# A RetNet and WaveMLP kernel on one core: the first half of a hand-written instruction order is laid out anew

## The chip, the cores and the metric

The kernel runs on one core of a Trainium2 chip. The metric is device time in microseconds for one execution. Before the change the median of three runs is 165.4 us (165.16 to 165.95). A core has five engines that run side by side, each through its own instruction list in order: TensorE (PE, matmuls and transposes into PSUM, with PEld for its weight loads), VectorE (DVE), ScalarE (ACT), GpSimd (POOL) and SyncE (SP). SP, ACT and POOL also issue DMA transfers.

## The reference

Two layers follow each other. The first is a linear recurrence with decay over 768 tokens, for 4 batches and 8 heads of 64 features; the second works on its output `x` of shape (4, 768, 512).

```python
for t in range(S):
    state = gamma * state + einsum('bhd,bhe->bhde', k[:, :, t], v[:, :, t])
    y[:, :, t] = scale * einsum('bhd,bhde->bhe', q[:, :, t], state)
...
theta = x @ w_theta
yr = einsum('ts,bsd->btd', w_tok_r, x * cos(theta))
yi = einsum('ts,bsd->btd', w_tok_i, x * sin(theta))
u = x + yr + yi
return u + maximum(u @ w_ch, 0.0)
```

Inputs and output are float32; the kernel multiplies in bfloat16 and sums in float32.

## The kernel before

The recurrence is computed in chunks of 128 tokens. The work is cut into 24 *units* n: a unit is half of the heads (4 of 8) and 256 tokens of one batch, so two units fill two chunks C of 128 tokens. Units 0 to 5 make batch 0, and so on. The 24 chunks also number the output tiles t.

The order of all instructions is written out by hand. `ORDER` is a string of 929 tokens such as `cqs.2.v`: a function's name, its numbers, and for many the engine (p POOL, v VectorE, a ACT) or the DMA queue (s SP, a ACT). The last lines of the kernel call the functions in that order, and each engine gets its instructions in the order in which they are called. An engine waits at an instruction until what it reads is there and the buffer that it writes is free. Nothing else moves instructions. The eight completion semaphores of the SP and ACT transfers are used in turn: the program makes each such transfer wait until the one eight places before it in the order has landed.

The steps of one unit n:

- `Lk`, `Lq`, `Lv` (L157) load k, q and v of the unit, 256 KB each, into 16 buffers for k and q and 9 for v.
- `ck` and `cq` or `cqs` (L302) turn k and q into bfloat16 `kqb`; `cqs` also scales q and is used for some units only. `cv` (L308) makes `vb`.
- `Tk`, `Tq` (L316) transpose both on TensorE, `E` copies the result out of PSUM as `kqT`. In later units `Dk` does the same by a DMA transpose.
- `A` (L346) multiplies keys and queries into `at_ps` (one buffer), `m` (L355, VectorE) applies the causal mask.
- `ST` (L373) adds up the unit's state change, `S0` and `S1` (L391, L395) keep the running state on VectorE, `SB` writes it as bfloat16 into block-diagonal tiles `sbd`.
- `I` (L411) takes the output from the older state, `Y` (L423) adds the one from inside the chunk, both into the PSUM banks of the next unit. `XB` and `XA` (L441) copy it out as `xT`.

The steps of the second layer, per chunk C or tile t:

- `Tx` (L455) with `Ex`, or `Dx`, turn `xT` into `x_sb`; `Hh` (L469) is the product with `w_theta`; `CN` (L476, ACT) takes sine and cosine; `z` (L483) multiplies them with `x`.
- `Tw` (L491) and `Ew` transpose the token-mixing weights, which `Pw` loads on POOL's queue in six pieces; `Pth` and `Pch` load the two other weights on the same queue, with a conversion to bfloat16 on the way.
- `M.t.s` (L509) is one pair of matmuls, and six such steps make a tile of `y`; `u` (L516) adds `x`; `Tu` and `Eu`, or `Du`, transpose; `O` (L536) is the product with `w_ch`; `f` (L542) finishes; `SO` stores.

`Z` (L278) is a filler: two matmuls of zeros whose result nobody reads.

The rotation of the PSUM buffers matters too: two banks for transposes, two for `th_ps`, `y_ps`, `o_ps` and the fillers, one for each half of the unit's output, and one for `at_ps`.

Of the kernel before, what the change touches and what calls it, by code (L numbers as in the profile page):

```python
# [29 lines left out]
ST.3 Lk.7.s S0.3.v SB.3.0.a S1.3 Lv.7.s Lk.8.s Tx.1 Tq.4 SB.3.1.p cv.4.p m.3 Pw.1.0 XB.2.0.a Ex.1.a  # L30
I.3 Lv.8.s E.4.a ck.5.a cq.5.a Y.3 Pw.0.0 ST.4 Hh.0 S0.4.v XB.3.0.v XB.3.1.v cv.5.v CN.0.1 A.4
CN.0.0 Tq.5 Hh.1 Tk.5 SB.4.0.p SB.4.1.a Pw.0.1 Hh.2 m.4 E.5.v I.4 Y.4 ST.5 ck.6.a Tk.6 Tx.2 cq.6.a
CN.1.1 CN.1.0 XA.4.1 A.5 XA.4.0 m.5 Lq.9.s Ex.2.v S0.5.v z.0.p Tq.6 E.6.a CN.2.0 cv.6.p Hh.3
SB.5.0.v Tx.3 Tw.1.0 z.1.v SB.5.1.a Ew.1.0.v Ex.3.a CN.2.1 A.6 I.5 Y.5 ST.6 XA.5.0 z.2.v Tw.0.0
CN.3.0 Tx.4 CN.3.1 Ew.0.0.v S0.6.v XA.5.1 Ex.4.v Hh.4 CN.4.0 CN.4.1 Tw.0.1 M.0.1 Pw.1.1 z.3.v M.0.0
Tw.0.2 Pw.1.2 Ew.0.2.a SB.6.1.a Hh.5 z.4.p SB.6.0.p Lk.9.a M.0.3 ck.7.p cqs.7.p M.0.2 CN.5.1 CN.5.0
cq.8.v m.6 Ew.0.1.v Tw.1.1 Tw.1.2 Ew.1.1.v Lv.9.s M.0.4 M.1.0 Tx.5 Ew.1.2.v M.1.1 S1.6 Tk.7 M.1.4
Pch Ex.5.v z.5.v cv.7.v Tq.8 Tq.7 M.1.2 E.7.a M.0.5 I.6 Y.6 ST.7 A.7 ck.8.a u.0 S0.7.v m.7 XA.6.1
SB.7.1.a M.1.5 M.1.3 XA.6.0 Tw.1.3 M.2.5 Pw.0.2 M.2.3 u.1 S1.7 Tk.8 M.2.1 M.2.0 SB.7.0.v Ew.1.3.a
Tu.0 I.7 cv.8.v E.8.a Lk.10.s ck.10.p cv.9.p Y.7 ST.8 A.8 cqs.9.v ck.9.v M.2.4 Du.1 Eu.0.a XB.7.1.a  # L40
XB.7.0.v S0.8.v SB.8.0.v M.2.2 Tx.6 Tq.9 Tk.9 Lv.10.a cv.10.p Lq.10.s S1.8 u.2 m.8 O.0 E.9.a
SB.8.1.a Hh.6 Tw.1.4 I.8 Y.8 A.9 CN.6.0 Du.2 Lq.14.s CN.6.1 Ex.6.v f.0 ST.9 Tw.0.3 Hh.7 Ew.1.4.v
Ew.0.3.a S0.9.v Tw.0.4 M.3.0 Tw.1.5 CN.7.0 CN.7.1 M.3.2 Dx.7 M.3.1 M.3.5 M.3.3 Lv.12.s Lk.12.s
Ew.1.5.v XA.8.1 Ew.0.4.v Lq.12.s M.3.4 u.3 S1.9 Tw.0.5 Tk.10 M.4.5 cqs.10.p XA.8.0 m.9 M.4.3 Tq.10
SB.9.1.a SB.9.0.a I.9 O.2 Lq.11.s Lk.11.s E.10.a Lk.15.s Ew.0.5.v Lk.14.s Y.9 ST.10 A.10 z.7.p
Lv.11.s XB.9.1.a XB.9.0.a f.2 M.4.0 O.1 M.4.1 cqs.14.p m.10 S0.10.v f.1 cq.11.a ck.12.v M.4.4 M.4.2
Tu.3 Eu.3.a Dx.9 SB.10.0.a cqs.12.p u.4 Hh.9 Tq.11 ck.11.v Tu.4 z.6.v Eu.4.v ck.15.v M.5.0 M.5.4
Tk.11 E.11.a SB.10.1.p cv.11.p M.5.2 M.5.3 I.10 M.5.5 M.5.1 Lq.13.a A.11 Y.10 ck.14.v ST.11 CN.9.1
CN.9.0 SO.0.a Hh.8 u.5 S0.11.v z.9.v XB.10.0.v m.11 Dk.12 Tx.8 Tq.14 O.4 Lv.13.a SB.11.0.a Lq.15.s
Lk.13.s CN.8.1 Lk.18.a XB.10.1.a CN.8.0 SB.11.1.p cv.12.p Lq.16.s I.11 Tk.14 Ex.8.v A.12 Y.11 ST.12  # L50
f.4 Lv.15.s O.3 z.8.p E.14.a XA.11.0 XA.11.1 Hh.10 S0.12.a f.3 SB.12.0.v Tx.10 Tu.5 CN.10.1 Dx.11
Ex.10.v cq.13.p Lk.16.s Lv.17.s Hh.11 SO.2.s CN.10.0 m.12 S1.12 z.10.v Tk.15 M.6.1 M.6.2 M.6.0 M.6.3
CN.11.0 CN.11.1 M.7.3 SB.12.1.a Lk.17.a ck.13.a M.7.4 M.7.0 M.6.4 Dk.13 M.7.1 z.11.v M.6.5 SO.3.s
A.14 M.7.2 Eu.5.v I.12 Lv.14.s u.6 cqs.15.v M.7.5 M.9.3 Tq.15 ck.17.a E.15.a m.14 SO.4.a Lq.17.s
Lq.18.s Lk.21.s ck.16.a M.9.0 M.9.5 M.9.1 M.9.4 Lq.19.a M.9.2 Du.6 cv.13.v u.7 M.8.0 u.9 Y.12
cv.14.p ST.13 A.13 O.5 XB.12.1.a XB.12.0.a M.8.1 S0.13.a S1.13 M.8.4 M.8.3 SB.13.0.a SB.13.1.p
cq.16.p m.13 I.13 ck.18.a Y.13 ST.14 A.15 f.5 cq.17.v Lv.18.a M.8.5 M.8.2 XA.13.0 XA.13.1 S0.14.v
SB.14.0.p Lv.16.s Hh.13 S1.14 u.8 Tx.12 M.10.1 cv.15.p cv.17.p SB.14.1.p M.10.0 M.10.4 cqs.18.v
M.10.5 CN.13.0 CN.13.1 Hh.12 CN.12.1 I.14 m.15 Y.14 CN.12.0 ST.15 S0.15.v XB.14.1.a SB.15.0.a M.10.3
cv.16.v Dk.16 Dk.17 Du.7 Dx.13 M.10.2 Dk.18 O.6 SB.15.1.p XB.14.0.v S1.15 I.15 Y.15 ST.16 SO.5.a  # L60
cv.18.p f.6 S0.16.v A.16 M.11.4 SB.16.1.p M.11.1 Lq.21.a Ex.12.a z.12.p SB.16.0.a Lk.19.s Lk.20.s
XB.15.0.a u.10 z.13.p XB.15.1.a m.16 O.7 Du.10 I.16 Y.16 ST.17 f.7 A.17 Tu.8 Hh.15 CN.15.1 CN.15.0
Dx.14 M.11.2 Tx.15 Lv.22.s SO.7.s M.11.0 M.11.5 S0.17.v SB.17.0.p M.11.3 XA.16.1 m.17 XA.16.0
Ex.15.v Hh.14 SB.17.1.p z.15.p cq.19.p ck.21.p Eu.8.a ck.19.p I.17 u.11 Tu.11 A.18 Y.17 ST.18
S0.18.v XA.17.1 XA.17.0 O.10 SO.1.a CN.14.1 S1.18 Lv.19.a CN.14.0 Dx.16 Lq.20.a f.10 Lq.22.a
SB.18.0.a Hh.17 SB.18.1.p Eu.11.v Tq.19 I.18 Tk.19 CN.17.1 O.8 Tx.17 CN.17.0 m.18 Hh.16 z.14.p
Lv.20.s Du.9 E.19.a f.8 O.11 Y.18 cv.19.p ck.20.a CN.16.1 ST.19 A.19 CN.16.0 M.12.1 Ex.17.v f.11
cq.20.p Lk.22.s Dk.20 M.12.0 S0.19.a M.13.3 M.13.2 XB.18.1.a SB.19.1.p SB.19.0.v M.13.0 z.17.v
cqs.21.v XB.18.0.v m.19 S1.19 z.16.v cv.20.v M.12.3 M.12.2 M.13.5 Lv.21.s M.13.1 M.12.4 M.12.5 I.19
M.13.4 Y.19 ST.20 u.12 A.20 Dk.21 XA.19.1 S0.20.v XA.19.0 ck.22.a cq.22.a SB.20.1.p cv.22.p M.14.3  # L70
M.14.5 M.14.1 M.14.4 M.14.2 M.14.0 SB.20.0.p u.13 m.20 S1.20 Hh.19 I.20 Y.20 SO.10.s Lq.23.s Lk.23.s
cv.21.v u.14 A.21 ST.21 CN.19.0 CN.19.1 S0.21.v M.15.3 M.15.5 S1.21 m.21 XA.20.1 Hh.18 CN.18.1
CN.18.0 Dx.18 Dk.22 ck.23.a M.15.4 M.15.2 SB.21.0.p M.15.1 M.15.0 SB.21.1.v Lv.23.s Du.12 Dx.19
XA.20.0 O.9 f.9 I.21 Y.21 A.22 ST.22 M.16.1 cqs.23.p u.15 m.22 S0.22.v z.18.p z.19.p M.16.5
SB.22.0.p M.16.4 O.12 M.16.0 SO.8.a M.16.2 M.16.3 SB.22.1.p XB.21.0.a XB.21.1.a SO.11.s Du.14
cv.23.p Dk.23 f.12 Du.13 Dx.20 Dx.21 Hh.21 u.16 I.22 A.23 Y.22 ST.23 CN.21.0 CN.21.1 Hh.20 CN.20.1
S0.23.v XA.22.1 XA.22.0 SB.23.0.a M.17.1 M.17.3 CN.20.0 M.17.0 SB.23.1.p I.23 M.17.2 m.23 Y.23 O.13
M.17.4 z.21.v M.17.5 Mh.0.1 Mh.0.3 XB.23.1.v f.13 Hh.23 u.17 XB.23.0.a SO.13.a CN.23.1 Du.16 Hh.22
z.20.v CN.22.1 Mh.0.2 M.19.3 Dx.23 CN.23.0 Dx.22 Mh.0.0 M.21.1 M.19.1 z.23.p CN.22.0 SO.6.a Du.17
M.18.1 O.16 M.21.2 M.19.2 M.19.0 M.18.3 f.16 SO.9.a M.18.5 z.22.p M.18.2 O.17 M.19.4 M.18.0 Mh.0.4  # L80
M.18.4 f.17 u.18 Du.15 SO.12.s O.15 M.19.5 f.15 u.19 SO.16.s M.22.2 M.22.1 O.14 Mh.0.5 uh.0 f.14
M.22.0 M.21.5 M.22.3 M.22.5 Du.19 M.21.4 SO.17.s M.22.4 Du.18 O.19 M.21.0 M.21.3 M.20.2 Mh.1.2
# [564 lines left out]
```

## Time and profile before

| what | value |
|---|---|
| median of three runs | 165.4 us |
| span of the profiled execution, first to last instruction | 163.6 us |
| TensorE busy | 155.2 us, 95% |
| VectorE busy | 114.0 us, 70% |
| ACT busy | 78.9 us, 48% |
| POOL busy | 74.3 us, 45% |
| bytes moved by DMA | 34.93 MB, 214 GB/s on average |
| read from and written to HBM | 25.69 MB and 6.29 MB |

The profile is of one execution. Its page gives each engine's busy time and share of the span, the busy share in 40 equal slices, the DMA queues, the chain of work that ended last, and the costliest groups of instructions. The trace behind the page answers finer questions: a timeline row has the start, the duration, the engine, the line, what is written and read, how many instructions were merged, and in brackets how long the engine stood idle before it and what released it. `SPq`, `ACTq` and `POOLq` are the issue of a DMA transfer. A row of the transfers has the tile, the queue, the count, the size and the time from issue to landing. Matmuls overlap, so the distance from start to start tells more of their cost than the duration.

### The profile page before, as it was taken

Reading aid. Unit: us, or ns where it says so; the run is one execution under the profiler, and the core shown is the slowest. Engines: PE = TensorE matmul, PEld = TensorE weight load, DVE = VectorE, ACT = ScalarE, POOL = GpSimd, SP = SyncE. Lnnn points to the kernel's source line nnn. Section 1 sums busy time; section 2 is a strip of 40 time slices with the busy share of each in tenths; the row PEclk is TensorE's granted clock in tenths of the full one; section 3 lists DMA queues with packets and bytes.
Section 4 is the critical chain, followed back from the end, with each engine's and each line's share of the span. In section 5 each row is a group of like instructions: output and inputs, shape, how many; then the busy total and the mean of one; then the engine's idle time right before and its main releaser. Section 6 shows DMA issues by size and latency. Waiting matters only on the chain.

```text
span 163.6 us, 4928 instructions
## 1 busy us (share of the span) xinstructions
PE 155.2 (95%) x2034; PEld 87.2 (53%) x2034; DVE 114.0 (70%) x215; ACT 78.9 (48%) x140; POOL 74.3 (45%) x107
## 2 busy tenths in 40 slices
...
GB/s 115 297 290 255 268 283 236 275 220 286 220 162 232 223 291 139 338 203 270 324 263 198 134 268 221 242 193 298 125 245 136 103 92 227 160 64 128 129 164 224
DMA packets 69062, 34.93 MB, mean 214 GB/s; under 512 B 26416, under 2 KB 66096, under 8 KB 69040
## 3 DMA queue, kind: packets, MB, share of 16 engines
q1 hardware_dynamic: 56032, 23.73, 69.4%
...
q0 software_dynamic: 2688, 3.41, 12.1%
q8 instruction: 16, 0.26, 0.7%
...
HBM read 25.69 MB, written 6.29 MB: 196 GB/s over the span
## 4 chain that ended last, share of the span: by engine, by line
PE 76%; DMA 8%; ACT 5%; POOL 3%; issue 2%; SPq 2%; DVE 1%; POOLq 0%; ACTq 0%
PE y_ps L509 36%; PE o_ps L536 11%; PE th_ps L469 10%; DMA kqf<-in_k_dram 8%; PE r_ps L423 3%; ACT qx L233 3%; PE w_ps L491 3%; PE at_ps L346 3%; PE r_ps L411 2%; PE kq_ps L316 2%; SPq L157 2%; PE y_ps L561 2%; ACT cs L476 1%; PE x_ps L455 1%; PE r_ps L373 1%
## 5 line engine op out<-in xcount | busy, mean ns | idle before, releaser
L509 PE MATMUL y_ps<-z,wtr 128*128 128x512 bf16 x138 | 52.4, 380 | 0.0
L509 PE MATMUL y_ps<-z,wti 128*128 128x512 bf16 x138 | 52.3, 379 | 0.0
L483 POOL TENSOR_TENSOR z<-cs,x_sb 128x1024 bf16<-128x1024 bf16 x12 | 25.5, 2136 | 17.9 <-ACT cs L476 10.0
L355 DVE TENSOR_TENSOR at<-at_ps,mask 128x1024 bf16<-128x1024 f32 x24 | 29.2, 1216 | 0.2
L469 PE MATMUL th_ps<-wth,xT 128*128 128x512 bf16 x96 | 24.5, 379 | 0.5 <-ACT cs L476 0.4
L516 DVE TENSOR_TENSOR u<-y_ps,x_sb 128x512 bf16<-128x512 f32 x23 | 15.8, 688 | 12.7 <-PE y_ps L509 12.6
L542 DVE SCALAR_TENSOR_TENSOR ot<-o_ps,u 128x512 f32<-128x512 f32 x22 | 15.1, 688 | 12.5 <-PE o_ps L536 12.4
L308 POOL TENSOR_TENSOR vb<-vf,vsc 128x512 bf16<-128x512 f32 x15 | 15.6, 1041 | 17.3 <-DMA vf<-in_v_dram 16.9
L476 ACT ACTIVATE cs<-th_ps,zerob 128x512 bf16<-128x512 f32 x24 | 16.4, 685 | 13.3 <-PE th_ps L469 8.8
L536 PE MATMUL o_ps<-wch,uT 128*128 128x512 bf16 x88 | 22.6, 379 | 0.0
L476 ACT ACTIVATE cs<-th_ps,halfpi 128x512 bf16<-128x512 f32 x24 | 16.3, 686 | 11.5 <-issue 5.4
L509 PEld LDWEIGHTS <-wtr 128*128 128x128 bf16 x138 | 13.5, 98 | 12.7
L509 PEld LDWEIGHTS <-wti 128*128 128x128 bf16 x138 | 13.5, 98 | 12.0 <-issue 0.2
L139 POOL CAST sbd<-s 64x256 bf16<-64x256 f32 (+1 forms) x21 | 10.1, 481 | 20.8 <-DVE s L391 17.7
L137 ACT COPY kqT<-kq_ps 128x1024 bf16<-128x1024 bf16 x12 | 12.1, 1012 | 11.9 <-PE kq_ps L316 11.9
L469 PEld LDWEIGHTS <-xT 128*128 128x128 bf16 x96 | 8.8, 98 | 8.7 <-issue 0.5
L137 ACT CAST kqb<-kqf 128x512 bf16<-128x512 f32 x16 | 9.6, 620 | 6.9 <-DMA kqf<-in_k_dram 6.3
L536 PEld LDWEIGHTS <-uT 128*128 128x128 bf16 x88 | 8.1, 98 | 8.3
L278 PE MATMUL zz<-zero 128*128 128x512 bf16 x30 | 10.3, 476 | 1.9 <-DVE zero L192 1.9
L423 PE MATMUL r_ps<-at,vb 64*64 64x128 bf16 x384 | 9.9, 221 | 1.6 <-DVE at L355 1.6
L316 PE MATMUL kq_ps<-ident,kqb 128*128 128x128 bf16 x120 | 11.2, 220 | 0.3 <-POOL kqb L302 0.3
L139 POOL CAST kqb<-kqf 128x512 bf16<-128x512 f32 x12 | 7.2, 612 | 8.5 <-DMA kqf<-in_k_dram 8.4
...
## 6 DMA issues: line engine op xcount, KB each, us to landing
vf<-in_v_dram SPq DMA_DIRECT2D x20, 256.0 KB, 5.9
kqf<-in_k_dram SPq DMA_DIRECT2D x19, 256.0 KB, 5.3
kqf<-in_q_dram SPq DMA_DIRECT2D x17, 256.0 KB, 5.8
out_dram<-ot ACTq DMA_DIRECT2D x12, 256.0 KB, 2.7
out_dram<-ot SPq DMA_DIRECT2D x11, 256.0 KB, 2.9
kqf<-in_q_dram ACTq DMA_DIRECT2D x7, 256.0 KB, 5.2
kqf<-in_k_dram ACTq DMA_DIRECT2D x5, 256.0 KB, 6.6
vf<-in_v_dram ACTq DMA_DIRECT2D x4, 256.0 KB, 5.8
```

Source lines behind the costliest of these rows:

```text
L137: nc.scalar.copy(dst, src)
L139: engines[e].tensor_copy(dst, src)
L308: engines[e].tensor_mul(in_blocks(vb), by_token(raw["vf", n]), _bcast_last(K["vsc"][:, i, :, h * HU:(h + 1) * HU], D))
L355: nc.vector.tensor_mul(at.rearrange("p g j a t -> p (g j) (a t)"), st["at_ps", n].rearrange("p g j a t -> p (g j) (a t)"), _bcast_mid(K["m ...
L423: nc.tensor.matmul(st["R", n + 1][c][g * D:(g + 1) * D, j * P:(j + 1) * P], st["vb", n][rows, lo:lo + D], st["at", n][rows, g, j, a, :], s ...
L469: nc.tensor.matmul(th_ps, st["xT", C][:, j, :], K["wth"][:, j, :], start=(j == 0), stop=(j == 3))
L476: nc.scalar.activation(st["cs", C][:, w, :], st["th_ps", C], AF.Sin, bias=K["zerob" if w else "halfpi"], scale=1.0)
L483: engines[e].tensor_mul(st["z", b][:, c], st["cs", C], _bcast_mid(x_of(C), 2))
L509: nc.tensor.matmul(st["y", t], K["wT"][r][:, s0, t0 * P:(t0 + 1) * P], st["z", b][:, s0, r, :], start=(done == 0 and r == 0), stop=(done = ...
L516: nc.vector.tensor_add(st["u", t], st["y", t], st["x", b][:, t0, :])
L536: nc.tensor.matmul(o_ps, st["uT", t][:, j, :], K["wch"][:, j, :], start=(j == 0), stop=(j == nD - 1))
L542: nc.vector.scalar_tensor_tensor(st["ot", t], st["o", t], 0.0, st["u", t], ALU.max, ALU.add)
```

## The change

The first 538 of the 929 tokens are put in a new order; the last 391, from `M.10.1` on, stay as they were. The same tokens stand in both halves, but 80 of them name another engine: the conversions, copies and products that may run on VectorE, ACT or POOL. The queue of each transfer is kept: a load that SP issued is still issued by SP, at another place in the order. The new order was laid out over a replay of the kernel in which the transfers of all queues are served in the order of their issue.

The beginning of the diff, up to unit 7 or so:

```diff
 const2 Lv.0.s const1 const6.v Z.29 Z.2 const5 Z.38 Lk.0.a const3 Z.35 Z.8 Lq.0.s Lv.1.s Z.28 constA
-const4 Lq.1.a const9 Lk.1.s Z.39 const8 ck.0.p Tk.0 ck.1.a cqs.0.v cv.0.p Tq.0 E.0.v Lq.4.a ST.0
-Lk.4.a cqs.1.p Tq.1 Lq.2.s S0.0.v SB.0.1.v A.0 Lk.2.s SB.0.0.p cv.1.p Lv.2.s S1.0 Z.15 I.0 Z.27 m.0
-Tk.1 E.1.a cqs.2.v Z.34 cv.2.p Y.0 ST.1 XB.0.1.a S0.1.v S1.1 SB.1.0.a Pth Lq.3.s Z.18 XB.0.0.v Tq.2
-A.1 SB.1.1.a ck.2.a I.1 m.1 Y.1 ST.2 Tk.2 const7 Z.23 XB.1.0.v Lk.3.s E.2.v XB.1.1.v A.2 ck.3.p
-S0.2.v m.2 S1.2 SB.2.1.a Z.11 cqs.3.p Tq.3 Lv.3.s Tx.0 Tk.3 Z.3 ck.4.p Lv.4.s Lk.5.s Lq.5.s Lv.5.s
-Lq.6.s Lk.6.s Lv.6.s Lq.7.s E.3.a SB.2.0.v I.2 Y.2 XB.2.1.a Ex.0.a cv.3.v cq.4.p Tk.4 Lq.8.s A.3
...
+const4 Lq.1.a const9 Lk.1.s cv.1.v Lk.2.s cv.0.p ck.1.a ck.0.p Z.39 ST.0 Tk.0 S0.0.v Lk.4.a cqs.0.v
+SB.0.0.v S1.0 Tq.0 E.0.a Lk.3.s Lq.2.s cqs.1.v Tq.1 ck.2.a A.0 cqs.2.p Tk.1 SB.0.1.v Pth I.0 Lq.4.a
+const8 ck.3.a Tk.2 Lq.5.s Z.18 m.0 const7 E.1.v Tq.2 ck.4.p Lq.3.s Y.0 E.2.v A.1 Z.34 ST.1 Z.23 m.1
+cqs.3.p Tk.4 XB.0.1.a XB.0.0.v Lv.3.s Lv.2.s cv.2.p S0.1.v Pw.1.0 A.2 Lk.5.s Z.11 Lv.4.s Tk.3 SB.1.0.a
+S1.1 SB.1.1.a Tq.3 cq.4.a I.1 Y.1 m.2 Lv.5.s ST.2 XB.1.1.v Tq.4 S0.2.v Lk.6.s S1.2 E.3.a XB.1.0.v Z.3
+SB.2.1.p cv.3.p Tx.1 A.3 Lq.6.s SB.2.0.a m.3 Lv.6.s Lq.7.s E.4.a Z.15 Ex.1.a I.2 Y.2 ST.3 cq.5.p Tx.0
+S0.3.v Hh.1 Lk.7.s SB.3.0.a SB.3.1.p S1.3 Pw.0.0 XB.2.0.v XB.2.1.v Hh.0 I.3 Y.3 CN.1.1 Ex.0.v cv.4.v
+ST.4 Pw.0.1 A.4 Tq.5 CN.1.0 Pw.1.1 ck.5.v Lv.7.s Tk.5 XB.3.0.v S0.4.v CN.0.0 cv.5.p m.4 XB.3.1.a
+SB.4.1.a Hh.2 E.5.a z.1.v SB.4.0.p Tx.2 I.4 Y.4 CN.0.1 ST.5 Pw.1.2 XA.4.0 Pw.0.2 ck.6.p S0.5.v Ex.2.a
+cq.6.a SB.5.1.p A.5 Tw.1.0 CN.2.1 Z.27 Lk.8.s Tk.6 XA.4.1 Tq.6 SB.5.0.p Ew.1.0.v Lq.8.s E.6.a Tx.3 m.5
...
+Ew.1.2.v cv.7.p ck.8.p Tq.7 z.4.v Tk.7 Tw.1.1 M.2.2 m.6 Lq.10.s SB.6.0.v M.2.1 M.2.0 M.0.4 M.2.5 M.2.4
+I.6 E.7.a Tw.1.4 Ew.1.1.a M.2.3 Tw.1.5 u.0 M.1.0 Lk.9.a M.1.1 cqs.9.p Ew.1.4.v Y.6 ST.7 A.7 Ew.1.5.a
+M.1.3 u.2 Tu.0 S0.7.v Tw.0.4 SB.7.0.a M.1.5 SB.7.1.v Lv.10.a Lq.11.s cq.8.a Eu.0.v Du.2 Tk.8 Ew.0.4.a
+Tq.8 cv.9.p M.1.2 S1.7 XA.6.1 I.7 M.4.2 cv.8.v E.8.a XA.6.0 M.1.4 m.7 u.1 Tw.0.3 M.4.1 M.4.3 Y.7 ST.8
...
```

The order in which the transfers are issued changes with it. Before, the loads of SP and ACT come as k0, v0, q0, v1, q1, k1, then q2, k2, v2, q3, k3, v3 with q4 and k4 on ACT's queue between them, then v4, k5. After, they come as k0, v0, q0, v1, q1, k1, k2, k3, q2, q5, q3, v3, v2, k5, v4 with k4 and q4 on ACT's queue. POOL issues `Pth` behind `cqs.2`, and five of the six `Pw` pieces within a few steps after `Pw.0.0`, `Pw.0.2` among them, which before came behind `Pch`.

More of the change, by code (lines that the diff above doesn't have):

```diff
@@ L29 @@
-Lq.6.s Lk.6.s Lv.6.s Lq.7.s E.3.a SB.2.0.v I.2 Y.2 XB.2.1.a Ex.0.a cv.3.v cq.4.p Tk.4 Lq.8.s A.3
[L30 to L82, printed above, removed]
```

50 lines of the change are left out of this document (46 added, 4 removed).

## The prediction

> **What bounds the kernel now.** I read the page first, then TensorE's order in time up to 30 us, then the busy time on both sides of the place where the two orders become equal, then the transfers.
>
> ```profile
> span 163.6 us, 4928 instructions
> PE 155.2 (95%) x2034; PEld 87.2 (53%) x2034; DVE 114.0 (70%) x215; ACT 78.9 (48%) x140; POOL 74.3 (45%) x107
> PE 76%; DMA 8%; ACT 5%; POOL 3%; issue 2%; SPq 2%; DVE 1%; POOLq 0%; ACTq 0%
> ```
>
> TensorE is busy for 95% of the span and holds 76% of the chain that ended last. The change only permutes work, so its gain can come only from gaps on TensorE. They all lie early:
>
> ```profile
> 7.34 0.61 PE L316 MATMUL kq_ps<-ident,kqb 128*128 128x128 bf16 x8
> ...
> 9.70 0.59 PE L278 MATMUL zz<-zero 128*128 128x512 bf16 x2
> 10.13 0.39 PE L316 MATMUL kq_ps<-ident,kqb 128*128 128x128 bf16 x4
> ...
> 13.86 0.42 PE L423 MATMUL r_ps<-at,vb 64*64 64x128 bf16 x16 [1.11 <-DVE at L355]
> ...
> 15.56 0.42 PE L346 MATMUL at_ps<-kqT 64*64 64x128 bf16 x16 [0.39 <-DVE kqT L139]
> ...
> 17.79 0.38 PE L411 MATMUL r_ps<-kqT,sbd 128*128 128x128 bf16 x4 [0.17 <-DVE sbd L139]
> 18.10 0.42 PE L423 MATMUL r_ps<-at,vb 64*64 64x128 bf16 x16
> 18.45 0.40 PE L316 MATMUL kq_ps<-ident,kqb 128*128 128x128 bf16 x4
> 18.78 0.42 PE L346 MATMUL at_ps<-kqT 64*64 64x128 bf16 x16
> 19.03 0.29 PE L373 MATMUL r_ps<-vb,kqb 64*64 64x64 bf16 x16
> 19.48 0.38 PE L455 MATMUL x_ps<-ident,xT 128*128 128x128 bf16 x4 [0.16 <-ACT x_sb L137]
> 19.70 0.39 PE L316 MATMUL kq_ps<-ident,kqb 128*128 128x128 bf16 x4
> 20.42 0.38 PE L411 MATMUL r_ps<-kqT,sbd 128*128 128x128 bf16 x4 [0.33 <-ACT xT L137]
> 21.27 0.42 PE L423 MATMUL r_ps<-at,vb 64*64 64x128 bf16 x16 [0.47 <-DVE at L355]
> 21.49 0.32 PE L373 MATMUL r_ps<-vb,kqb 64*64 64x64 bf16 x16
> 21.75 1.04 PE L469 MATMUL th_ps<-wth,xT 128*128 128x512 bf16 x4
> ...
> 26.94 0.40 PE L316 MATMUL kq_ps<-ident,kqb 128*128 128x128 bf16 x4
> 27.72 1.02 PE L469 MATMUL th_ps<-wth,xT 128*128 128x512 bf16 x4 [0.39 <-ACT cs L476]
> ```
>
> ```profile
> 28.63:87.06 58.43, 58.34 (x829) 34.55 (x828) 46.50 (x93) 32.99 (x58) 22.28 (x25) 1.00 1.22 246
> ```
>
> The first answer shows the real matmuls starting at 7.34, ahead of them only seven filler steps (Z). The seven gaps marked from 13.86 on sum to 1.11 + 0.39 + 0.17 + 0.16 + 0.33 + 0.47 + 0.39 = 3.02 us. The second has one stage, from 28.63 to 87.06, where the common tail of the two orders begins (token M.10.1): TensorE busy 58.34 of 58.43 us, at the full granted clock (1.00). Were all seven gaps gone, the gain would be 3 us. The loads are what the early gaps depend on:
>
> ```profile
> 1.86 0.50 SPq L157 DMA_DIRECT2D vf<-in_v_dram  x1
> vf<-in_v_dram SPq DMA_DIRECT2D x1, 256.0 KB, 6.1
> ...
> 9.32 6.61 DMA kqf<-in_k_dram
> ...
> 15.94 0.37 SPq L157
> ...
> 12.62 0.93 POOL L173 DMA_DIRECT2D wth<-in_moe_w_theta_dram  x1
> wth<-in_moe_w_theta_dram POOLq DMA_DIRECT2D x1, 512.0 KB, 6.8
> q1 hardware_dynamic: 56032, 23.73, 69.4%
> q0 software_dynamic: 2688, 3.41, 12.1%
> ```
>
> Lv.1, fifth load in the order of issue, lands at 1.86 + 6.1 = 7.96. Lk.4, the fourteenth, issued by ACT at 9.32, lands at 15.93. That is (15.93 - 7.96) / 9 = 0.89 us a load, so the transfers are a second full resource. The step after it shows the limit on depth: SP issues Lk.5 at 15.94, as the load eight places before it has landed. Weights cost more: queue 0 takes 12.1 / 3.41 = 3.55% a MB, queue 1 takes 69.4 / 23.73 = 2.92%, or 1.21 times as much, so Pth (512 KB) occupies the engines for 2 x 0.89 x 1.21 = 2.2 us.
>
> **The change, part by part.** *Conversions moved between engines.* No matmul, copy or load is added; 80 copies and products change engine and both halves hold the same 14 filler steps. TensorE sees only when operands are ready, so I price waits.
>
> *Start.* VectorE's first product is now cv.1 and its second work on unit 0 comes behind it; cqs.0 used to be first.
>
> ```profile
> 6.22 0.69 DVE L302 TENSOR_TENSOR kqb<-kqf,qsc 128x512 bf16<-128x512 f32 x1 [3.26 <-DMA kqf<-in_q_dram]
> 10.56 1.01 ACT L137 COPY kqT<-kq_ps 128x1024 bf16<-128x1024 bf16 x1 [1.09 <-PE kq_ps L316]
> 11.63 1.04 POOL L308 TENSOR_TENSOR vb<-vf,vsc 128x512 bf16<-128x512 f32 x1 [1.34 <-DMA vf<-in_v_dram]
> 8.85 0.62 ACT L137 CAST kqb<-kqf 128x512 bf16<-128x512 f32 x1
> ```
>
> VectorE must sit until Lv.1 at 7.96, is done with cv.1 at 8.65 (0.69 us for that shape), copies S0.0 and ends cqs.0 near 9.5. Tq.0 thus starts near 9.6 where TensorE is free near 7.8: some 1.7 us idle, and 0.8 us more until Tq.1 behind cqs.1. E.0 moves to ACT: 10.0 to 11.0. This start alone isn't the cost, because fillers stand in the old order there (Z.15 and Z.27 have run by 10.13) and later chains bind; it counts through the ledger below.
>
> *Loads.* Lv.2 goes from ninth to fourteenth place, Lq.4 from twelfth to fifteenth: ACT issues it behind ck.2, which stands behind E.0, so near 11.0. Pth keeps its time: cqs.2 on POOL needs Lq.2, ninth, at 7.96 + 4 x 0.89 = 11.5, takes 1.05 and frees POOL at 12.6. Then POOL does ck.4, cqs.3 and cv.2. Served in order, Lv.2 lands at 15.93 and cv.2 ends at 15.95 + 1.04 = 17.0; Lq.4 lands at 15.93 + 0.89 = 16.8. If Pth goes ahead of them, both slip by up to its 2.2 us: Lq.4 to 19.0. Which end is nearer is shown by another load issued just before POOL's transfers:
>
> ```profile
> 20.86 1.10 SPq L157 DMA_DIRECT2D kqf<-in_q_dram  x1
> kqf<-in_q_dram SPq DMA_DIRECT2D x1, 256.0 KB, 9.7
> 21.28 0.60 POOL L182 DMA_DIRECT2D row<-in_moe_w_tok_i_dram  x1
> ```
>
> Lq.7, 0.4 us ahead of three weight transfers, took 9.7 us, not 6.1: it was overtaken. Lq.4 would have 1.6 us of lead over Pth, so I take a little over half of the slip: 18.1.
>
> The Trainium skill (DMA: Bandwidth & Descriptors, Queues, rings and completion order) states that each DMA engine takes turns between the queue rows that have work, a packet at a time, which speaks against an order laid out over service in issue order. By that rule Lq.4, alone on ACT's row, would pass Lv.2, and Lv.2 would share with Pth and land near 18.1: cv.2 to 19.15, ST.2, Tq.4, Z.3 and Tx.1 behind it, A.3 near 20.3, an estimate 0.5 us worse than mine. Lq.7's row agrees for POOL's queue; for SP against ACT the even 0.89 us steps don't show it.
>
> *Who waits for Lq.4.* ACT holds cq.4, then E.3, then SB.2.0; A.3 on TensorE waits for E.3. cq.4 runs 18.15 to 18.8, E.3 to 19.8, A.3 starts at 19.85. Before it started at 18.78. TensorE has done less by then: the order puts Z.15, Z.27, I.2 and Y.2 after A.3, Tq.4 before it. From start to start a Z takes 10.13 - 9.70 = 0.43, I.2 0.31, Y.2 0.35, a Tk or Tq 0.33: 0.86 + 0.31 + 0.35 - 0.33 = 1.19 us. So the new order is 1.07 + 1.19 = 2.26 us behind at A.3.
>
> *What it wins back.* The gaps after 18.78 in the old order, start to start: ST.3 to Tx.1 0.45 where 0.26 is needed (21.49 to 21.75), Tq.4 to I.3 0.72 for 0.33, I.3 to Y.3 0.85 for 0.31, Tq.6 to Hh.3 0.78 for 0.33: 0.19 + 0.39 + 0.54 + 0.45 = 1.57. The new order sets Tx.0, Hh.1 and Hh.0 before I.3, two groups of four long matmuls (21.75 to 22.71 is one, 0.96 us), which cover the two largest. I leave 0.2 us of loss (0 if the cover is whole, 1.57 if nothing is covered).
>
> **Sum:** 2.26 - 1.57 + 0.2 = +0.9 us on a span of 163.6; nothing after 87.06 differs but the start time. The median 165.4 lies 1.8 us over that span and keeps its distance: 166.3.
>
> **The rivals.**
> *Served in issue order, faster.* Lq.4 at 16.8 gives cq.4 to 17.45, E.3 to 18.45, A.3 at 18.5: -0.28 + 1.19 - 1.57 = -0.66 with no loss left, so 164.7; with the 0.2 us tightening elsewhere that the rows can't tell, 164.5. For it: the fourteen even landings, of both queues. Against it: Lq.7's 9.7 us. It decides at a landing of Lq.4 before about 17.
> *Weights drawn ahead starve unit 8, clearly slower.* Pw.0.2 (576 KB) is now issued before Lk.8, Pch (512 KB) soon after.
>
> ```profile
> 27.08 0.97 SPq L157 DMA_DIRECT2D kqf<-in_k_dram  x1
> kqf<-in_k_dram SPq DMA_DIRECT2D x1, 256.0 KB, 12.7
> ...
> 38.26 0.61 PE L316 MATMUL kq_ps<-ident,kqb 128*128 128x128 bf16 x8
> ```
>
> Lk.8 landed at 39.8 behind the same loads as Lq.8 in the new order; Pw.0.2 adds 2.25 x 0.89 x 1.21 = 2.4 us, Pch up to 2.2: 42.2 to 44.4. TensorE ran Tq.8 at 38.26; the new order has about 6 us more ahead of it (eight M steps net, 0.43 each, and ten short ones), so with 0.9 us of delay it comes at 45 and cq.8 needs the load by 44.4. It decides from there; some 1.7 us late gives 168.0. For it: 12.7 us for one load. Against: the margin, 0 to 2 us.
> *Nothing comes of it.* The start's loss and the cover cancel (the slip of Lq.4 is 0.4 of Pth's): 165.4.
>
> **How the numbers follow.** Forecast 0.48, own range 164.7 to 167.2 (Lq.4 in order, or wholly behind Pth); in order 0.26; starved 0.17; nothing 0.09. A measurement of this kernel tells about 0.5%, 0.8 us, from no change. The forecast lies just beyond it: 0.31 slower, 0.17 same. In order: 0.17 faster, 0.09 same; starved: slower; nothing: same. Slower 0.48, same 0.35, faster 0.17. The range 164.3 to 168.1 takes in both sides.
>
> **What would show it.** Tq.0 idle until about 9.6 behind VectorE's cv.1; Lq.4 landing near 18; cq.4 or E.3 as the releaser ahead of A.3 near 19.9; no gaps from 20 to 28; M.10.1 starting near 88.0. Wrong if Lq.4 lands before 17, if a gap over 0.5 us stands before Tq.8, or if M.10.1 comes before 87.

## The result: slower by 0.6%, and the profile after

The changed kernel takes 166.74 us (median of five, 166.41 to 166.78); the ratio to the kernel before is 1.0059, 95% interval [1.0037, 1.0082]. The forecast was 166.3 us. The two medians, 165.4 and 166.74, are 1.3 us apart, the two profiled spans 1.4. All ratios go by the faster state of the executions; in `e10_all_early` seven of twelve, at 168.3 to 168.6 us and at a granted clock of 0.99 to 1.00, fell out as slow, so its ratio may flatter it and stands alone. Lines in `kernel.py` are two lower than before (the loads L155, `ck`/`cq` L135 or L137, `cqs` L300, `cv` L306, `Tk`/`Tq` L314, `A` L344, `ST` L371, `Y` L421).

First the page of the changed kernel: the span, the engines' busy times, the granted clock in 40 slices, and the queue that brings instructions (transfers, MB, share), which is needed near the end.

```profile
span 165.0 us, 4914 instructions
PE 154.0 (93%) x2005; PEld 87.6 (53%) x2034; DVE 112.1 (68%) x211; ACT 78.7 (48%) x138; POOL 77.8 (47%) x113
PEclk9978999999999999999999999999999999999998
q8 instruction: 16, 0.26, 0.7%
```

TensorE's busy time is 1.2 us less over a span that is 1.4 us longer, but 29 of its 2,034 matmul records are missing, so this difference proves little. The work is the same by construction. Where TensorE loses time is shown by its order in time, each row with start, duration, line, tiles and, in brackets, the idle time and what ended it:

```profile
9.47 0.40 PE L314 MATMUL kq_ps<-ident,kqb 128*128 128x128 bf16 x4 [1.22 <-DVE kqb L300]
10.39 0.51 PE L314 MATMUL kq_ps<-ident,kqb 128*128 128x128 bf16 x4 [0.53 <-DVE kqb L300]
...
18.89 0.39 PE L453 MATMUL x_ps<-ident,xT 128*128 128x128 bf16 x4
19.21 0.42 PE L344 MATMUL at_ps<-kqT 64*64 64x128 bf16 x16
...
32.87 0.28 PE L453 MATMUL x_ps<-ident,xT 128*128 128x128 bf16 x2 [0.77 <-issue]
...
45.94 0.40 PE L314 MATMUL kq_ps<-ident,kqb 128*128 128x128 bf16 x4 [0.86 <-ACT kqb L135]
```

Two gaps at the start (Tq.0, Tq.1), A.3 at 19.21 with no wait marked before it, then a gap in the middle of Tx.4 that no semaphore explains, and one before Tq.8. The one before Tq.8 ends with cq.8 on ACT, and the chain of waits, cut at 50 us and followed back, says what cq.8 waited for (start, duration, what):

```profile
26.00 19.25 DMA kqf<-in_q_dram
45.27 0.63 ACT kqb L135
45.94 0.40 PE kq_ps L314 x4
```

Lq.8 was on its way for 19.25 us. The transfers that SP and POOL issued around it, as rows of the transfers (tile, queue, count, size, us from issue to landing):

```profile
kqf<-in_k_dram SPq DMA_DIRECT2D x1, 256.0 KB, 16.7
row<-in_moe_w_tok_r_dram POOLq DMA_DIRECT2D x1, 576.0 KB, 14.2
kqf<-in_q_dram SPq DMA_DIRECT2D x1, 256.0 KB, 19.2
wch<-in_moe_w_ch_dram POOLq DMA_DIRECT2D x1, 512.0 KB, 11.2
```

These are Lk.8 (issued at 25.46, landed at 42.2), Pw.0.2 (26.18, 40.4), Lq.8 (26.00, 45.2) and Pch (33.23, 44.4). Pch was issued 7 us after Lq.8 and landed 0.8 us before it (44.4 against 45.2).

A ledger says what each stage cost. For every TensorE step I take the distance from the start of its first matmul to the next such start, less the distance that this kind of step needs where nothing waits (M and Z 0.43, Hh and O 0.86, Tw 0.335, A, Y and ST 0.235, the others 0.22, an I of two matmuls 0.11), and add up from 6.5 us:

```
TensorE time lost since 6.5 us, at the start of   A.3    A.6    M.0.1  Tq.8   M.10.1 (starts at)
before                                            4.08   6.72   7.26   7.29   8.73   (87.06)
after                                             5.61   6.82   7.88   9.05   10.16  (88.50)
```

The change is 1.53 us behind at A.3 and has made up all but 0.10 us by A.6, at 30 us. The order of the small steps differs, so such a difference is sure to 0.1 or 0.2 us only. Between A.6 and Tq.8 the change loses 2.23 us where the kernel before lost 0.57: 0.94 at Tx.4's gap and 1.03 at Tq.8's. From Tq.8 to M.10.1 it loses 1.11 where the kernel before lost 1.44. The sum, 0.10 + 1.66 - 0.33 = 1.43 us, is the delay of M.10.1 (88.50 - 87.06), and behind M.10.1 both take the same 76.5 us.

### The profile page after: what moved, and what is told of

Read it like the earlier page. It is cut to its first block, busy times and chain, and to the rows that moved or that the text cites. A ratio compares the mean times of both kernels' runs of the same rounds, so it can differ in the third digit from the quotient of the medians.

```text
span 165.0 us, 4914 instructions
## 1 busy us (share of the span) xinstructions
PE 154.0 (93%) x2005; PEld 87.6 (53%) x2034; DVE 112.1 (68%) x211; ACT 78.7 (48%) x138; POOL 77.8 (47%) x113
## 4 chain that ended last, share of the span: by engine, by line
PE 74%; DMA 15%; POOL 3%; issue 2%; DVE 2%; ACT 2%; SPq 1%; POOLq 0%; DVEq 0%; ACTq 0%
PE y_ps L507 31%; DMA kqf<-in_q_dram 12%; PE o_ps L534 11%; PE th_ps L467 10%; PE r_ps L421 4%; PE kq_ps L314 4%; DMA vf<-in_v_dram 4%; PE at_ps L344 3%; PE r_ps L409 3%; PE y_ps L559 2%; PE r_ps L371 2%; PE zz L276 2%; PE x_ps L453 1%; POOL z L481 1%; POOL kqb L137 1%
## 5 line engine op out<-in xcount | busy, mean ns | idle before, releaser
L507 PE MATMUL y_ps<-z,wtr 128*128 128x512 bf16 x133 | 50.5, 380 | 0.5
L507 PE MATMUL y_ps<-z,wti 128*128 128x512 bf16 x126 | 47.8, 379 | 0.8 <-issue 0.6
L481 POOL TENSOR_TENSOR z<-cs,x_sb 128x1024 bf16<-128x1024 bf16 x11 | 23.4, 2134 | 10.1 <-ACT cs L474 9.9
L306 POOL TENSOR_TENSOR vb<-vf,vsc 128x512 bf16<-128x512 f32 x17 | 18.0, 1061 | 13.0 <-DMA vf<-in_v_dram 8.4
L467 PE MATMUL th_ps<-wth,xT 128*128 128x512 bf16 x90 | 23.7, 379 | 0.3
L137 POOL CAST sbd<-s 64x256 bf16<-64x256 f32 (+1 forms) x23 | 10.5, 456 | 27.9 <-DVE s L389 27.0
L135 ACT CAST kqb<-kqf 128x512 bf16<-128x512 f32 x19 | 11.6, 624 | 5.5 <-DMA kqf<-in_k_dram 4.1
L314 PE MATMUL kq_ps<-ident,kqb 128*128 128x128 bf16 x120 | 11.4, 230 | 2.8 <-DVE kqb L300 1.8
L300 POOL TENSOR_TENSOR kqb<-kqf,qsc 128x512 bf16<-128x512 f32 x8 | 8.8, 1094 | 8.8 <-DMA kqf<-in_q_dram 8.8
L135 ACT COPY kqT<-kq_ps 128x1024 bf16<-128x1024 bf16 x11 | 11.1, 1011 | 3.7 <-PE kq_ps L314 3.6
L314 PEld LDWEIGHTS <-kqb 128*128 128x128 bf16 x120 | 8.5, 103 | 6.9 <-DVE kqb L300 2.1
```

Of the source, the lines that this page charges most:

```text
L135: nc.scalar.copy(dst, src)
L306: engines[e].tensor_mul(in_blocks(vb), by_token(raw["vf", n]), _bcast_last(K["vsc"][:, i, :, h * HU:(h + 1) * HU], D))
L314: nc.tensor.transpose(st["kq_ps", n][:, 4 * w + x, :], st["kqb", n][:, w, x * P:(x + 1) * P], K["ident"])
L467: nc.tensor.matmul(th_ps, st["xT", C][:, j, :], K["wth"][:, j, :], start=(j == 0), stop=(j == 3))
L481: engines[e].tensor_mul(st["z", b][:, c], st["cs", C], _bcast_mid(x_of(C), 2))
L507: nc.tensor.matmul(st["y", t], K["wT"][r][:, s0, t0 * P:(t0 + 1) * P], st["z", b][:, s0, r, :], start=(done == 0 and r == 0), stop=(done = ...
```

## The experiments

Theory A, formed on these rows: the weight transfers Pw.0.2 and Pch, drawn ahead, starve unit 8's loads. The edits are moves of tokens in `ORDER`.

**One transfer moved.** `e1_pch_later` puts Pch behind cv.7:

```diff
-z.5.v Tw.1.2 cqs.7.p Lq.9.s Pch Lv.9.s ck.7.a ... cv.7.p ck.8.p Tq.7
+z.5.v Tw.1.2 cqs.7.p Lq.9.s Lv.9.s ck.7.a ... cv.7.p Pch ck.8.p Tq.7
```

> Pch is issued behind cv.7 instead of ahead of it, some 5 us later (near 39 us instead of 33.2); all else as in the changed kernel (median 166.74, span 165.0, Lq.8 landing at 45.24, 0.9 us of idle TensorE before Tq.8). Theory A (weights drawn ahead of unit 8's loads make Lq.8 late): Lq.8 lands near 43.2, the gap before Tq.8 goes, the time falls by 0.9 to 1.2 us to about 165.7. Rival B (the transfers as a whole set the pace, so another load takes Lq.8's place): Lq.8 lands earlier but a gap of the same size opens elsewhere before 60 us, for O.0 or a later unit, and the time stays within 0.3 us of 166.74.

Measured: 166.07 us, ratio 1.0041 [1.0013, 1.0069], executions from 165.06 to 167.48. Lq.8, in the rows of the transfers of this kernel (issued at 25.84), and Pch (39.66):

```profile
kqf<-in_q_dram SPq DMA_DIRECT2D x1, 256.0 KB, 15.7
wch<-in_moe_w_ch_dram POOLq DMA_DIRECT2D x1, 512.0 KB, 8.7
```

Lq.8 lands at 41.6 instead of 45.2, Tq.8 follows Tk.8 without a wait, and M.10.1 starts at 87.72. The starving is shown: one transfer taken out of Lq.8's way gives it 3.5 us. The other runs repeat it. In the four profiles with this order's engines and Pch at its early place (the changed kernel, e2, e3, e4) Lq.8 lands at 45.0 to 45.7 and Tq.8 waits 0.86 to 1.67 us; in the six with Pch later (e1, e5, e9 to e12) it lands at 41.2 to 41.8 and Tq.8 doesn't wait. What that is worth in time is not as sure: the interval overlaps that of `e4_after_again` below, and the median is above the 165.7 that theory A had forecast.

**The start.** `e2_cqs0_first` puts cv.1 behind cqs.1 on VectorE; `e3_fillers_early` puts three fillers into TensorE's first gaps; `e4_after_again` is the changed kernel once more.

```diff
 e2
-Lk.1.s cv.1.v Lk.2.s ... cqs.0.v ... cqs.1.v Tq.1
+Lk.1.s Lk.2.s ... cqs.0.v ... cqs.1.v cv.1.v Tq.1
 e3
-Tk.0 S0.0.v ... Tq.0 E.0.a ... Z.18 ... Z.34 ... Z.23
+Tk.0 Z.18 Z.34 S0.0.v ... Tq.0 Z.23 E.0.a
```

> cv.1 goes behind cqs.1 on VectorE, so that cqs.0 no longer waits behind Lv.1. The two gaps of 1.2 and 0.5 us before Tq.0 and Tq.1 should go in either theory and the granted clock should stay at 1.00 from 10 to 14 us, where it was 0.50. Theory C (the loss at the start is carried to the end): A.3 starts about 1 us earlier than 19.2, M.10.1 too, and the time falls by about 1 us to 165.7. Rival D (the loss at the start is absorbed before 31 us, since both orders are equally far there; what costs is later): A.3 moves by less than 0.5 us and the time by less than 0.4 us.

> The fillers Z.18 and Z.34 go into the gap before Tq.0 and Z.23 into the one before Tq.1, from behind Tk.2 and A.1; the wait for cqs.0 stays. If idle TensorE is what lowers the granted clock, the clock stays at 1.00 from 10 to 14 us. Theory C': the half clock delays the unit chain (Tq.2, Y.0, A.1) and its end is worth 0.5 us or more, time 166.2 or less. Rival D': the chain is bound by VectorE and the loads there, or what is won is absorbed by 31 us, time within 0.3 us of 166.74.

> The changed kernel once more, unchanged, beside the others. The 0.77 us of idle TensorE in the middle of Tx.4 at 32.1 us had no releaser in the profile. If it belongs to the order (a fixed place in TensorE's instruction stream), it stands again at the same instruction with 0.5 us or more; if it was chance, it is gone or stands elsewhere. The time is 166.4 to 166.8 either way.

Measured: e2 166.78, ratio 1.0086 [1.0063, 1.0109]; e3 166.76, 1.0072 [1.0046, 1.0099]; e4 166.64, 1.0063 [1.0042, 1.0084]. In e2 Tq.0 starts at 8.31 instead of 9.47, with gaps of 0.66 and 0.53 us left before Tq.0 and Tq.1, and A.3 still at 19.20; in e3 A.3 comes at 19.58. The start as such is absorbed. The clock was 1.00 from 10 to 14 us in both, as expected, but in e3 it was 0.50 from 15.2 to 18.5 instead, and e1 kept 1.00 with the old start, so nothing is shown about what the fillers do to the clock. e4 gives the same two late gaps in other sizes, 0.34 us at Tx.4 (less than the 0.5 forecast) and 1.40 before Tq.8, and M.10.1 at 88.31.

**Lv.2.** What holds TensorE before A.3 in e1 is ST.2, waiting for cv.2, and so for Lv.2, now in fourteenth place:

```profile
18.11 0.32 PE L371 MATMUL r_ps<-vb,kqb 64*64 64x64 bf16 x16 [0.99 <-POOL vb L306]
```

`e5_lv2_early` is e1 with Lv.2 issued three places earlier.

```diff
-ck.3.a Tk.2 Lq.5.s ... Lq.3.s ... Lv.3.s Lv.2.s cv.2.p
+ck.3.a Tk.2 Lv.2.s Lq.5.s ... Lq.3.s ... Lv.3.s cv.2.p
```

> This is the kernel of e1_pch_later with one more load moved: SyncE issues Lv.2 ahead of Lq.5, Lq.3 and Lv.3, in place of behind them. Theory (what holds ST.2 and A.3 in the changed kernel is Lv.2's late place among the loads, landing at 16.81): Lv.2 now lands at 13.5 to 15, the first product of A.3 starts at 18.4 to 18.9 in place of 19.21. What that is worth: if early lateness persists, the median is 165.1 to 165.4 (0.7 below e1); rival (lateness of that stage is made up by 30 us, because the loads of units 4 to 6 or the weights of that stage bind anyway): the ledger is level with e1 again by A.6 and the median stays within 0.3 of 166.07.

Measured: 167.02, ratio 1.0114 [1.0077, 1.0152]. Lv.2 lands at 12.3 and the wait is gone, but A.3 starts at 19.14 against e1's 19.34 and A.6 at 29.84 against 29.99, and 0.16 us of that lead was there at Tk.0 already (7.27 against 7.43). So taking the wait away bought next to nothing, as the rival said, but not for the rival's reason, and the median isn't within 0.3 of e1's as the rival had it. The granted clock of the two kernels from 10 to 14 us (stretch, length, busy time of PE, PEld, DVE, ACT and POOL, then the clock, the DMA share and GB/s), e1:

```profile
10.00:14.00 4.00, 3.23 (x69) 2.00 (x70) 3.05 (x6) 3.98 (x8) 1.91 (x2) 1.00 1.22 290
```

and e5:

```profile
10.00:14.00 4.00, 3.50 (x60) 2.44 (x64) 2.84 (x5) 3.98 (x8) 1.92 (x2) 0.71 1.22 290
12.00:15.00 3.00, 3.00 (x42) 1.53 (x40) 2.46 (x4) 2.98 (x5) 1.96 (x3) 0.50 1.22 290
```

In e5 TensorE ran at half its clock from 12 to 15 us and reached A.2 later than in e1, e5 first:

```profile
16.24 0.42 PE L344 MATMUL at_ps<-kqT 64*64 64x128 bf16 x16
```

```profile
15.26 0.42 PE L344 MATMUL at_ps<-kqT 64*64 64x128 bf16 x16
```

The dip cost the microsecond that Lv.2 gave. The changed kernel had the same dip (0.57 over 10 to 14). There TensorE came to ST.2 at 17.98 without a wait, just when cv.2 had ended (17.92), so the dip and Lv.2 would each have set that time alone. In the profile e5 falls behind e1 at O.0, which waited 0.76 us for Pch (landed at 49.2).

**Order and engines apart.** `e6_old_engines` is the new order with the 80 tokens' old engines, `e7_new_engines_old_order` the reverse.

```diff
 e6
-cv.1.v Lk.2.s cv.0.p ... E.0.a ... cqs.1.v
+cv.1.p Lk.2.s cv.0.v ... E.0.v ... cqs.1.p
```

> The new order with the vector steps on the engines that they had before (80 steps given back their old engine; order, loads and weights as in the changed kernel). Theory A (the loss is the order of the transfers: Pw.0.2 and Pch ahead of unit 8's loads): Lq.8 still lands at 44.5 to 46, a gap of 0.5 to 1.7 us before Tq.8 remains, and the median is 166.4 to 167.2. Rival (the loss is that engines were swapped, VectorE and ScalarE changing places in the early chain): the median comes back to 165.2 to 165.8 and the clock dip of the first stage goes with it.

> The order of before with the vector steps on the engines of the changed kernel. Theory A: Lk.8 lands near 40 and Pw.0.2 near 49 as before, no gap before Tk.8 or Tq.8, and the median is 165.1 to 165.8, the same as before. Rival (the swap of engines costs by itself): 166.2 or more, with VectorE's cv.1 again holding Tq.0 for about 1.2 us at 9.5.

Measured: e6 180.0, ratio 1.0885 [1.0861, 1.0908]; e7 184.24, 1.1145 [1.1112, 1.1178]. Both theories fell: neither half can be had alone, and the 0.6% can't be shared out between them. Nor does e6 test theory A, since POOL came to Pw.0.2 at 28.96 instead of 26.18 and Lq.8 landed at 31.7. One large piece of e6 is readable, VectorE's and POOL's order in time:

```profile
29.98 4.46 DVE L481 TENSOR_TENSOR z<-cs,x_sb 128x1024 bf16<-128x1024 bf16 x1
```

```profile
29.76 2.13 POOL L481 TENSOR_TENSOR z<-cs,x_sb 128x1024 bf16<-128x1024 bf16 x1
31.84 1.05 POOL L306 TENSOR_TENSOR vb<-vf,vsc 128x512 bf16<-128x512 f32 x1
32.84 1.04 POOL L300 TENSOR_TENSOR kqb<-kqf,qsc 128x512 bf16<-128x512 f32 x1
33.83 0.81 POOL L174 DMA_DIRECT2D wch<-in_moe_w_ch_dram  x1
```

and TensorE's Tk.6 behind it:

```profile
35.45 1.01 PE L314 MATMUL kq_ps<-ident,kqb 128*128 128x128 bf16 x8 [4.04 <-DVE x_sb L137]
```

The same product takes VectorE 0.68 us (median of its 12 here). It ended at 34.44, after POOL's three products, and Tk.6 waited 4.04 us for a copy behind it on VectorE. That agrees with the Trainium skill (SBUF — State Buffer, SBUF: two separate sides), by which VectorE and GpSimd share one port pair that is held for a whole instruction. Why VectorE was passed over between POOL's products, too, isn't shown. I didn't follow e7's many small waits.

**The weights in the old order.** `e8_weights_ahead_old` is the kernel before with Pw.0.2 and Pch issued straight behind Pw.1.2, and nothing else changed.

```diff
-Tw.0.2 Pw.1.2 Ew.0.2.a ... Pch ... Pw.0.2
+Tw.0.2 Pw.1.2 Pw.0.2 Pch Ew.0.2.a
```

> The kernel before, with one thing of the change alone: POOL's transfers Pw.0.2 and then Pch are issued straight behind Pw.1.2 in place of some 10 us later. Theory A (weights ahead of unit 8's loads starve unit 8): Lk.8, which landed at 39.8, lands at 42 to 44.5, a gap of 0.5 to 2.4 us appears before Tk.8 or Tq.8, and the median is 165.9 to 167.5. Rival (weights and loads overtake each other without harm, the gap in the changed kernel has another cause): no such gap, median within 0.3 of 165.4.

Measured: 168.5, ratio 1.0185 [1.0147, 1.0224]. Lk.8 lands at 41.84 and is still in time; the load behind it is not. Lv.8, as a row of the transfers, and ST.8 in TensorE's order:

```profile
vf<-in_v_dram SPq DMA_DIRECT2D x1, 256.0 KB, 17.7
```

```profile
46.78 0.32 PE L371 MATMUL r_ps<-vb,kqb 64*64 64x64 bf16 x16 [2.00 <-DVE vb L306]
```

Theory A holds in the old order too, through Lv.8 and not Lk.8. The median is 3.1 us above that of the kernel before beside it (165.43) and above the range forecast; 2.0 us of it are this wait.

**Can e1 be mended?** In e1 Pch lands just when O.0 needs it. `e9_o0_later` moves O.0 behind Hh.7, `e11_o0_between` only behind S1.8, and `e10_all_early` adds e2's and e5's edits to e9.

```diff
 e9
-XB.7.0.a Ew.0.3.a O.0 M.4.5 m.8 M.4.4 f.0 ... Hh.7 cq.11.a ... Tx.6 I.8
+XB.7.0.a Ew.0.3.a M.4.5 m.8 M.4.4 ... Hh.7 O.0 cq.11.a ... Tx.6 f.0 I.8
 e11
-XB.7.0.a Ew.0.3.a O.0 M.4.5 m.8 M.4.4 f.0 ... S1.8 Lk.11.s Lq.12.s Hh.6 Lv.11.s
+XB.7.0.a Ew.0.3.a M.4.5 m.8 M.4.4 ... S1.8 O.0 Lk.11.s Lq.12.s Hh.6 f.0 Lv.11.s
```

> The kernel of e1_pch_later (Pch moved behind cv.7.p), and the first product that needs Pch, O.0, with its eviction f.0, moved about 3 us later in TensorE's order, behind Hh.7. Theory (in e1 and e5 Pch lands at 48.4 to 49.2, just when O.0 is due, and some executions wait for it, which is where e1's scatter from 165.06 to 167.48 comes from): no wait for wch before O.0, the executions lie within 1 us of each other, and the median is 165.4 to 165.8. Rival (the scatter and the remaining 0.6 have another cause): the scatter stays over 1.5 us and the median is 165.9 to 166.4.

> The kernel of e9 with both causes of the late start taken away together: cv.1 behind cqs.1 on VectorE (as in e2) and Lv.2 ahead of Lq.5 (as in e5). Theory (each of the two alone was hidden by the other or by Lq.4): Tq.0 starts near 8.2, A.3 near 18.4 to 18.9 in place of 19.2, and the lead lasts: median 164.8 to 165.3, below before. Rival (PE's lateness before 30 us is absorbed whatever it is, since units 4 to 6 come when their loads land): M.0.1 at 31.9 to 32.3 as in e1 and e5, median level with e9 within 0.3.

> The kernel of e1_pch_later with O.0 moved only behind S1.8 (about 2 us later in TensorE's order, ahead of Hh.6) and f.0 behind Hh.6. Theory (e9 lost its gain to a new wait, O.0 for ScalarE's cs behind Hh.7, 0.6 us; between the two places neither wch nor cs is late): no wait of over 0.2 us at o_ps, median 165.4 to 165.8, scatter under 1.2 us. Rival (the remaining distance to before is in small losses spread over TensorE's order after 50 us, not in these waits): the wait at o_ps is gone and the median still is 166.0 to 166.4.

Measured: e9 166.3, ratio 1.0048 [1.0026, 1.0071], executions within 1.0 us; e10 ratio 1.0047 [1.0013, 1.0082]; e11 166.87, 1.0090 [1.0062, 1.0118]. In e9 O.0 now waits for ScalarE:

```profile
52.91 1.02 PE L534 MATMUL o_ps<-wch,uT 128*128 128x512 bf16 x4 [0.55 <-ACT cs L474]
```

So e9's scatter is as the theory said and its median is not. In e11 neither wait is left, and it is the slowest of the three: two gaps stand in its TensorE order for which the profile shows no releaser.

```profile
32.40 0.29 PE L453 MATMUL x_ps<-ident,xT 128*128 128x128 bf16 x2 [0.50 <-issue]
...
60.28 0.38 PE L507 MATMUL y_ps<-z,wtr 128*128 128x512 bf16 x1 [0.99 <-issue]
```

The first is the gap inside Tx.4 again, the second stands in M.3.3. It is there, at 0.2 to 1.0 us, in e1, e5, e10, e11 and e12, and in none of the profiles with Pch early. e10 has A.3 at 19.06, with the clock at 0.67 from 10 to 14 us. None of the three beats the kernel before.

**Neither Lv.2 nor the dip.** `e12_no_dip` is e11 with Lv.2 early and two fillers in the first gaps.

```diff
-Tk.0 S0.0.v ... Tq.0 E.0.a ... Lq.5.s Z.18 ... Z.34 ... Lv.3.s Lv.2.s
+Tk.0 Z.18 S0.0.v ... Tq.0 Z.34 E.0.a ... Lv.2.s Lq.5.s ... Lv.3.s
```

> The kernel of e11 with Lv.2 early (as in e5) and with two of TensorE's filler steps moved into its idle time at the start, Z.18 ahead of Tq.0 and Z.34 ahead of Tq.1. In e5, e10 and the profile of e11 the granted clock was 0.50 from about 12 to 15 us, in e1 and e9 it was 1.00, and A.3 stood at 19.06 to 19.34 in all of them. Theory (two covers lie over each other: the clock's dip costs about 1 us by A.2, and the wait for Lv.2 costs about 1 us at ST.2; either alone sets A.3): with neither, the clock is 1.00 from 10 to 16 us, A.3 starts at 18.2 to 18.7, and the median is 0.5 to 0.9 below e11, 166.0 to 166.4. Rival (the loads of units 3 and 4 set A.3 whatever comes before): A.3 at 19.0 to 19.4 again and the median level with e11 within 0.3.

Measured: 170.32, ratio 1.0262 [1.0209, 1.0314]. The theory is right about A.3 and wrong about the time. The clock and A.3:

```profile
10.00:14.00 4.00, 3.08 (x84) 2.07 (x84) 3.05 (x6) 3.98 (x8) 1.91 (x2) 1.00 1.22 290
39.80:43.00 3.20, 2.98 (x8) 1.06 (x7) 2.11 (x4) 1.14 (x2) 2.54 (x3) 0.50 1.19 291
```

```profile
18.46 0.42 PE L344 MATMUL at_ps<-kqT 64*64 64x128 bf16 x16
...
38.22 0.40 PE L314 MATMUL kq_ps<-ident,kqb 128*128 128x128 bf16 x4 [2.22 <-ACT kqb L135]
```

A.3 starts at 18.46, the only one of the new orders below 19. But now Tk.7 waits for Lk.7, and idle time is followed by half the clock a second time: the five M steps from 39.39 to 43.23 take 3.84 us instead of 2.15, 1.7 us more. Why Lk.7 is late shows in POOL's and SP's issues and in the rows of the transfers (Lq.7, Lk.7), e12:

```profile
21.19 1.32 POOL L180 DMA_DIRECT2D row<-in_moe_w_tok_r_dram  x2
22.49 0.78 POOL L180 DMA_DIRECT2D row<-in_moe_w_tok_i_dram  x1
```

```profile
20.98 1.93 SPq L155 DMA_DIRECT2D kqf<-in_q_dram  x1
22.95 1.17 SPq L155 DMA_DIRECT2D kqf<-in_k_dram  x1
```

```profile
kqf<-in_q_dram SPq DMA_DIRECT2D x1, 256.0 KB, 11.5
kqf<-in_k_dram SPq DMA_DIRECT2D x1, 256.0 KB, 14.6
```

and e11:

```profile
21.88 1.32 POOL L180 DMA_DIRECT2D row<-in_moe_w_tok_r_dram  x2
23.18 0.74 POOL L180 DMA_DIRECT2D row<-in_moe_w_tok_i_dram  x1
```

```profile
20.87 1.04 SPq L155 DMA_DIRECT2D kqf<-in_q_dram  x1
21.95 1.47 SPq L155 DMA_DIRECT2D kqf<-in_k_dram  x1
```

```profile
kqf<-in_q_dram SPq DMA_DIRECT2D x1, 256.0 KB, 6.3
kqf<-in_k_dram SPq DMA_DIRECT2D x1, 256.0 KB, 11.1
```

POOL came to its weights 0.7 us sooner (21.19 against 21.88), as A.3 did (18.46 against 19.12). Its three weights left from 0.2 us after Lq.7 on, instead of 1.0, and all ahead of Lk.7, where in e11 only the first did. Lq.7 then took 11.5 us instead of 6.3, and Lk.7, issued 1.0 us later, landed at 37.5 instead of 33.0. e5 and e10 lie between: with the weights 0.97 and 0.78 us behind Lq.7, Lk.7 landed at 33.6 and 34.8. What was won at the front was lost to transfers that overtook.

## Why the prediction was right in size and wrong in its place

- *The start.* Tq.0 was to start near 9.6 behind cv.1, Tq.1 0.8 us later: 9.47 and 10.39, released by VectorE's `kqb`. Right, and, as the prediction also said, not a cost by itself (e2).
- *Lq.4 at 18.1: the step that failed.* It was issued at 9.91 and not near 11.0, since ACT put the transfer out before ck.2, which stands ahead of it in the order. So it had 2.6 us of lead over Pth (12.49) and not 1.6, and of the 1.3 us by which Pth was to delay it nothing came: it took 6.4 us and landed at 16.32. "Wrong if Lq.4 lands before 17" was met. A.3 was nevertheless late, at 19.21 against the 19.85 forecast and 18.78 before, for other reasons: half the clock from 10.5 to 14.0 us, and Lv.2 (16.81, cv.2 until 17.92), which would have held TensorE as long.
- *The rule of the Trainium skill* (DMA: Bandwidth & Descriptors, Queues, rings and completion order). By it Lq.4 on ACT's row would pass Lv.2 on SP's: it did, 16.32 against 16.81, though issued 0.18 us later. Lv.2 was to be held by Pth until 18.1 and was not. For POOL's row against SP's the rule's direction is borne out by Lq.8 and by e12.
- *2.26 us behind at A.3, 1.37 won back.* By the ledger 1.53 behind (5.61 - 4.08), and 1.43 won back by 30 us. The cover by Hh.0 and Hh.1 was sized well. The loss was too large by 0.73 us, so what the forecast's own sum adds up came out as +0.1 us in place of +0.9.
- *No gaps from 20 to 28.* None over 0.22 us. Right.
- *M.10.1 near 88.0: the other step that failed.* The sum has no term between 30 us and M.10.1, and there 1.33 us were lost (1.66 - 0.33). M.10.1 starts at 88.50, so that the number fits is luck: the delay came by the second rival, given 0.17 (1.03 us at Tq.8), and by the gap in Tx.4 (0.94), which no rival had, less what the kernel before lost elsewhere. For the second rival the prediction had the numbers, 42.2 to 44.4 for the load that takes Lk.8's old place, now Lq.8 (45.2), and Tq.8 at 45 needing it by 44.4; its margin of "0 to 2 us" was -0.8. Lateness was priced at 1.7 us and the wait was 0.86. "Wrong if a gap over 0.5 us stands before Tq.8" was met, too.
- *The first rival* was to decide at Lq.4 before 17, with 164.5 to 164.7. Its condition came true and its time did not: A.3 came at 19.21 and not 18.5, because Lq.4 was not the last load that mattered.

Shown: Pch, drawn ahead, makes Lq.8 late (the rows of Lq.8 and e1), and both weights together make Lv.8 late in the old order (e8); Pw.0.2 alone was not moved. Also shown: the early loss is absorbed by 30 us, and A.3 is held by Lv.2 or by the clock, whichever is there (e1, e5, e12). Not shown is that Pch is the whole 0.6%: every order with Pch moved is still slower than the kernel before. e1's M.10.1 comes 0.66 us later than before, with no wait over 0.5 us between 20 us and there. By the ledger 0.08 of it is lost by Tq.8, 0.20 by O.0, and the rest behind O.0, where the gap in M.3.3 stands (0.2 us of it).

Not settled: why Tx.4 stops. The gap stands at the same place in 6 of the 10 profiles that keep the new order's engines (the changed kernel, e2, e4, e9, e10, e11), at 0.34 to 0.77 us, and the kernel before has none; in the changed kernel it makes over half of the 1.66 us lost from A.6 to Tq.8. What the traces do show is the place. TensorE's list has 4,090 instructions in a complete trace (e11: 2,034 weight loads, as many matmuls, 22 others), and queue q8 brings 16 transfers of 0.26 MB in all, 16 KB each: some 256 instructions to a transfer. In program order, counted behind the two that open the program and with the semaphore instructions among them, 703 instructions stand ahead of a gap in Y.4 (0.22 us at 26.39), 959 ahead of the one in Tx.4 and 1,727 ahead of the one in M.3.3. These are 256 and 768 apart, so all three gaps stand at the same place of such a block, as its border would. That points to the supply of instructions and not to a step of the kernel. Why TensorE stops at some of these places, in some executions, and at none in the kernel before stays open.
